# Attention and two feed-forward stages on one core: attention in the order of token thirds, with a table of times, and four pairs loaded in 1 KB runs

## The chip, the cores and the metric

One Trainium2 chip, one of its cores. The metric is the device time of one execution in microseconds. The kernel before was run three times; the median is 508.46 us (507.33 to 509.16).

## What is computed

Attention over q, k, v of shape (2, 8, 576, 64), float32, in two branches that are added. One averages q, k and v over groups of four tokens, does full softmax attention on 144 of them, and repeats each result four times. The other is local: each token sees the tokens less than 4 away. The sum, as 1152 tokens of 512 values, goes through two feed-forward stages, whose weights are float64 or float32 as the inputs have them:

```python
out = out_up + out_local                       # (2, 8, 576, 64)
x = out.transpose(0, 2, 1, 3).reshape(1152, 512)
h = x @ w_in                                   # 512 -> 2048
g = h * np.tanh(softplus(h))
y = g @ w_out                                  # 2048 -> 512
g2 = silu(y @ w_gate) * (y @ w_val)            # 512 -> 1536, twice
return g2 @ w_out2                             # 1536 -> 512
```

## The kernel before

**Names.** PE is TensorE, ACT ScalarE, DVE VectorE, POOL GpSimd, SP the engine that issues the transfers. Heads go in pairs: (b, p) is batch b, heads 2p and 2p + 1, eight pairs in all.

**The planner.** Nothing is issued in the order of the source. Each step is an `Op` with the engines that may do it and a guessed duration on each, the steps that it needs, the ring buffers that it takes, and a wanted time. `Plan.run` (line 97) plays the engines through in its own clock: an engine that is free takes, of the steps that are ready, the one with the smallest wanted time. The order found in this way is then issued, engine by engine, and each engine works through its own list in order. A wanted time is a priority and no time on the chip. Where PE has nothing ready before 95 us of the plan's clock, a dummy matmul (line 1082) is put in its list; it computes nothing that is used.

**prep** (line 396) takes one pair in. Tokens 0 to 511 of q and of k are loaded (lines 414 to 423) in runs of 256 B, so that one partition holds four neighbouring tokens of both heads, ordered token, head, value. The last 64 tokens come once for each batch (`ld_rem`, line 389), v in 1 KB runs (line 427), and POOL adds groups of four v rows (line 440). `t_main` (line 449) transposes four blocks of 128 x 128 for q and four for k (line 456), ACT evicts them (line 473), and DVE adds groups of four tokens (line 484). A branch for 1 KB runs stands in the code (lines 420 and 458 to 461) for batches named in `KB`, which is empty: one run holds four tokens of one head, and each block is a plain multiplication of one head's 64 columns with the identity.

**down** (line 505) is the averaged branch of one pair: score (520), maxima (525), exponentials on ACT (535), the scaling of the exponentials on ACT or DVE (548, 550), transposes (559), values (571). Its result goes to `up`.

**load_windows** (line 598) loads v for the local branch, a window of 70 tokens of four heads at a time (line 604), 36 in all.

**duo** (line 608) is the local branch of two units. A unit is (b, u, p): batch, third of its 576 tokens, pair. There are 24 units and 12 duos. Mask and scores (631, 636), maxima on DVE (642), exponentials on ACT (650), their sums either by ACT's accumulator or, with `late_sums`, by DVE (655), scaling (668), transposes (676), values (691). Then DVE adds the averaged branch (line 701), the sum is rounded to its high part (707) and the low part is taken (711); both go to `xt`.

**The first layer.** `convert` (line 265) loads one chunk of 512 KB of float64 weights and makes a high and a low float32 part of it: an absolute value on ACT or DVE (297, 299), four steps on DVE (303, 307, 312, 317), the high part on either (224 and 226 are the copy helper), the low part on DVE (333). `l1` (line 780) multiplies one chunk with one piece of 384 tokens (`cols_group`, 12 matmuls on lines 756 to 758). A piece is two thirds: piece 0 is the first two thirds of batch 0, piece 1 the last third of batch 0 and the first of batch 1, piece 2 the rest. An `l1` group needs every unit of its piece. For the first six chunks the three pieces are separate groups whose results are kept; `l2`, `l3` and `l4` follow in a fixed order.

**The order around the change** (lines 971 to 1050). `w` counts up by 4 a duo. The twelve duos are, by (b, u, p): 000+010, 001+011, 020+021, 002+012, 003+013, 022+023, 100+101, 110+120, 111+121, 102+103, 112+122, 113+123. Piece 0 so is complete after the fifth, piece 1 after the tenth, piece 2 after the twelfth. The first five have `late_sums`. Windows are asked for nine at a time. The weights' first conversion is wanted at

```python
    for f in range(WTS):
        convert("1", f, t_p0 + 4.5 * f, -4)
```

with t_p0 = 30, and `l1` of pieces 0, 1 and 2 from 40, 60 and 58 on.

Of the kernel before, what the change touches and what calls it, by code (L numbers as in the profile page):

```python
# [29 lines left out]
KB = ()  # L30
# [137 lines left out]
def attention_moe_kernel(  # L168
# [96 lines left out]
    def convert(kind, f, want, lead=None):  # L265
# [24 lines left out]
        if wide:  # L290
# [29 lines left out]
            o = plan.add({"ACT": us_act(512), "DVE": us_ts(512)}, mag, [o_load, prev.get("mag")], w0, [cw], [raw])  # L320
# [75 lines left out]
    def prep(b, p, w):  # L396
# [17 lines left out]
        def ld_main(i):  # L414
            def f(e):
# [33 lines left out]
        def t_main(i):  # L449
            def f(e):  # L450
# [3 lines left out]
                for r in range(4):  # L454
                    if b not in KB:
# [13 lines left out]
        def ev(i):  # L469
            def f(e):  # L470

                if i < 2:
# [16 lines left out]
        for i in range(3):  # L489
            o = plan.add({E_PE: ((1.06 if b in KB else 0.5) if i < 2 else 0.24)}, t_main(i) if i < 2 else t_rem,  # L490
# [4 lines left out]
            evs.append(plan.add({"ACT": us_act(n, True), **({} if 7 & 1 else {"DVE": us_tt(n)})}, ev(i), [o], w, use=[ps[i], qkT]))  # L495
# [4 lines left out]
        pairs[b, p] = dict(qkT=qkT, evs=evs, o_up=down(b, p, qkd, vd, o_d, o_v, w + 9.04+0.00))  # L500
# [4 lines left out]
    def down(b, p, qkd, vd, o_d, o_v, w):  # L505
# [37 lines left out]
        def weigh(h):  # L543
            def f(e):
                for c in range(2):
                    t, r = ed.tile[:, h, c], md.tile[:, 0, h, c:c + 1]
                    if e == "ACT":
                        ACT.activation(t, t, AF.Copy, scale=r)
                    else:
                        DVE.tensor_scalar(out=t, in0=t, scalar1=r, scalar2=None, op0=ALU.mult)  # L550
# [28 lines left out]
        o = add({E_PE: 0.54}, score, o_d, w, ba + [ed, md], [qkd])  # L579
        o = [add({"DVE": us_tt(2 * SD)}, mx(h), [o], w, use=[ba[h], md]) for h in range(2)]  # L580
        o = add({"DVE": 0.08}, neg, o, w, use=[md])
        o = add({"ACT": 1.25}, exps, [o], w, use=ba + [md, ed], table="exp")
        o = add({"DVE": 0.25}, norm, [o], w, use=[md])
        o_e = []
        for h in range(2):
            x = add({"ACT": 0.42, "DVE": 0.29}, weigh(h), [o], w, use=[md, ed])
            x = add({E_PE: 0.3}, turn(h), [x], w, [] if h else [ptd], [ed, ba[h]] + ([ptd] if h else []))
            o_e.append(add({"ACT": us_act(2 * SD, True)}, ev(h), [x] + o_e, w, use=[ba[h], ptd]))
        o = add({E_PE: 0.5}, values, o_e + o_v, w, use=[vd, ptd, ba[0]])
# [18 lines left out]
    def duo(units, ws, late_sums):  # L608
# [11 lines left out]
        xs = buf(wk, [128, 384], F32, "xs", 2)  # L620
        b_s, b_l = [bank() for _ in two], [bank() for _ in two]
        b_o = bank()

# [60 lines left out]
        def o_local(k):  # L684
            def f(e):
                if k == 0:
                    b_o.make()
                    xs.make()
                for j in range(3):
                    for h in range(2):  # L690
                        PE.matmul(out=b_o.tile[64 * h:64 * h + 64, 192 * k + 64 * j:192 * k + 64 * j + 64], lhsT=vw[k][j].tile[:, 2 * (units[k][2] % 2) + h],  # L691
                                  rhs=pt[k].tile[:, 128 * j + 64 * h:128 * j + 64 * h + 64], start=True, stop=True)
# [11 lines left out]

        hi, lo = [xt[:, z, p0:p0 + np_, 192 * s0:192 * (s0 + ns)] for z in range(2)]

        def x_hi(e):
            copy(e, hi, xs.tile.rearrange("p (c j) -> p c j", c=np_))

        def x_lo(e):  # L710
            DVE.tensor_tensor(out=lo, in0=xs.tile.rearrange("p (c j) -> p c j", c=np_), in1=hi.bitcast(F32), op=ALU.subtract)
# [7 lines left out]
        for k in two:  # L719
            pr, w, u = prs_[k], ws[k], units[k][1]  # L720
            o1 = add({E_PE: 0.66}, s_local(k), pr["evs"][:2 + (u == 2)] + [o_bf] + in_turn[-1:], w,
# [3 lines left out]
            o6.append(add({"ACT": 0.45 if late_sums else 0.92}, exps(k), [o3], w, [], [b_s[k], m, ex], "exp"))  # L725
# [15 lines left out]
        for k in two:  # L741
            o15.append(add({E_PE: 0.48}, o_local(k), [o12[k]] + o15 + l_w[k], w, [] if k else [b_o, xs],
                           [pt[k]] + vw[k] + ([b_o, xs] if k else [])))
        o17 = add({"DVE": us_tt(384)}, add_, o15 + [prs_[k]["o_up"] for k in two], w, use=[b_o, up, xs])
# [374 lines left out]
```

## Time and profile before

| what | us |
|---|---|
| median of three runs | 508.46 |
| the profiled execution's own time | 508.12 |
| its span, first to last instruction | 506.3 |
| PE recorded busy | 500.4 |
| DVE recorded busy | 351.3 |
| ACT recorded busy | 270.5 |

Times inside a profile count from the span's start. A matmul's recorded duration holds its way through the array, so durations of matmuls that follow one another overlap, and a stretch full of dummies is as busy as a stretch full of work. Where PE's true pace matters, it is read from how many instructions lie between two starts, or from the chain of waits, which counts no microsecond twice. A share of DMA is that of the 16 transfer engines.

### The profile page before, as it was taken

What the parts mean: (1) busy time and instruction counts of PE and PEld (TensorE: products, weight loads), DVE (VectorE), ACT (ScalarE), POOL (GpSimd) and SP (SyncE); (2) the same over time, 40 slices, a digit from 0 to 9 for tenths busy, and PEclk for the clock granted to TensorE, in tenths of its full rate; (3) what the DMA queues carried; (4) which work ended last, traced back from release to release, by engine and by line L of the source; (5) the groups of instructions that cost most, each with busy time, mean ns of one, the idle gap of its engine ahead of it and who ended that gap; (6) DMA issues with size and microseconds to landing.
All of it is one profiled execution on the core that took longest, in us unless ns stands there. A gap on an engine that the chain in (4) does not pass through costs nothing.

```text
span 506.3 us, 8742 instructions
## 1 busy us (share of the span) xinstructions
PE 500.4 (99%) x3387; PEld 469.3 (93%) x3387; DVE 351.3 (69%) x743; ACT 270.5 (53%) x602; POOL 24.7 (5%) x45
## 2 busy tenths in 40 slices
PE   9999999999999999999999999999999999999996
PEld 7777779999999999999999999999998899998885
DVE  3898999986966982877598986776763298622322
ACT  3989998699968860897053533344432444310000
POOL 4432220000000000000000000000000000000000
PEclk9999999999999999999999999999999999999999
DMA  9999533440451540045114252222222032000022
GB/s 174 197 168 220 147 102 101 149 132 15 123 174 34 167 128 39 1 126 167 41 43 124 88 162 85 85 83 85 83 84 83 1 124 84 1 1 0 1 96 90
DMA packets 58225, 48.23 MB, mean 95 GB/s; under 512 B 30664, under 2 KB 53448, under 8 KB 58184
## 3 DMA queue, kind: packets, MB, share of 16 engines
q1 hardware_dynamic: 58184, 47.68, 34.4%
q8 instruction: 26, 0.43, 0.4%
q14 instruction: 15, 0.12, 0.1%
HBM read 45.31 MB, written 2.36 MB: 94 GB/s over the span
## 4 chain that ended last, share of the span: by engine, by line
PE 91%; DVE 4%; ACT 3%; issue 1%; ACTq 0%
PE b L756 23%; PE b L757 23%; PE b L758 23%; PE b L943 5%; PE b L941 5%; PE b L942 5%; PE warm L1082 2%; PE b L691 1%; PE b L636 1%; PE b L456 1%; PE b L676 1%; DVE qkd L484 1%; ACT ex L650 1%; ACT ed L535 1%; PE b L520 1%
## 5 line engine op out<-in xcount | busy, mean ns | idle before, releaser
L756 PE MATMUL b<-xy,wt 128*128 128x384 f32 x480 | 161.2, 336 | 0.0
L758 PE MATMUL b<-xy,wt 128*128 128x384 f32 x480 | 160.4, 334 | 0.0
L757 PE MATMUL b<-xy,wt 128*128 128x384 f32 x480 | 160.4, 334 | 0.0
L756 PEld LDWEIGHTS b<-xy,wt 128*128 128x128 f32 x480 | 90.1, 188 | 0.4
L757 PEld LDWEIGHTS b<-xy,wt 128*128 128x128 f32 x480 | 90.1, 188 | 0.0
L758 PEld LDWEIGHTS b<-xy,wt 128*128 128x128 f32 x480 | 90.1, 188 | 0.0
L756 PE MATMUL b<-G,wt 128*128 128x384 f32 x192 | 64.1, 334 | 0.0
L757 PE MATMUL b<-G,wt 128*128 128x384 f32 x192 | 64.1, 334 | 0.0
L758 PE MATMUL b<-G,wt 128*128 128x384 f32 x192 | 64.1, 334 | 0.0
L224 ACT ACTIVATE G<-H 128x384 fp32r<-128x384 f32 (+1 forms) x38 | 21.7, 576 | 65.4 <-DVE H L913 44.5
L297 ACT ACTIVATE cw<-raw 128x512 f32<-128x512 f32 x65 | 43.7, 673 | 21.0 <-DVE wt L333 12.7
L333 DVE TENSOR_TENSOR wt<-cw,wt 128x512 fp32r<-128x512 f32 x68 | 46.2, 686 | 3.7 <-ACT wt L224 2.0
L312 DVE SCALAR_TENSOR_TENSOR cw<-raw,cw 128x512 uint32<-128x512 uint32 x68 | 46.5, 690 | 0.8
L317 DVE SCALAR_TENSOR_TENSOR cw<-raw,cw 128x512 uint32<-128x512 uint32 x68 | 46.5, 688 | 0.5
L943 PE MATMUL b<-wt,G 128*128 128x512 f32 x108 | 42.1, 389 | 0.0
L942 PE MATMUL b<-wt,G 128*128 128x512 f32 x108 | 42.0, 389 | 0.0
L941 PE MATMUL b<-wt,G 128*128 128x512 f32 x108 | 42.0, 389 | 0.0
L913 DVE TENSOR_TENSOR H<-b,H 128x384 f32<-128x384 f32 x36 | 19.9, 553 | 24.8 <-PE b L758 24.6
L956 DVE TENSOR_TENSOR acc<-b,acc 128x512 f32<-128x512 f32 x18 | 12.4, 692 | 34.6 <-PE b L943 34.6
L756 PEld LDWEIGHTS b<-G,wt 128*128 128x128 f32 x192 | 36.0, 188 | 0.0
L757 PEld LDWEIGHTS b<-G,wt 128*128 128x128 f32 x192 | 36.0, 188 | 0.0
L758 PEld LDWEIGHTS b<-G,wt 128*128 128x128 f32 x192 | 36.0, 188 | 0.0
(91 smaller groups left out, 690.2 us busy)
## 6 DMA issues: line engine op xcount, KB each, us to landing
raw<-in_moe_w_out_dram SPq DMA_DIRECT2D x28, 512.0 KB
raw<-in_moe_w_in_dram SPq DMA_DIRECT2D x16, 512.0 KB
raw<-in_moe_w_gate_dram SPq DMA_DIRECT2D x12, 512.0 KB
raw<-in_moe_w_val_dram SPq DMA_DIRECT2D x12, 512.0 KB
vw<-in_v_dram SPq DMA_DIRECT2D x36, 70.0 KB
vq<-in_v_dram SPq DMA_DIRECT2D x8, 288.0 KB
out_dram<-acc SPq DMA_DIRECT2D x9, 256.0 KB
qk<-in_q_dram SPq DMA_DIRECT2D x8, 256.0 KB
```

Source lines behind the costliest of these rows:

```text
L224: ACT.activation(out, in_, AF.Copy)
L297: ACT.activation(cw.tile, h.bitcast(F32), AF.Abs)
L312: DVE.scalar_tensor_tensor(out=c, in0=words()[:, :, 0], scalar=29, in1=c, op0=ALU.logical_shift_right, op1=ALU.bitwise_or)
L317: DVE.scalar_tensor_tensor(out=c, in0=words()[:, :, 1], scalar=0xC0000000, in1=c, op0=ALU.bitwise_and, op1=ALU.bitwise_or)
L333: DVE.tensor_tensor(out=wt.tile[:, 1], in0=cw.tile, in1=wt.tile[:, 0].bitcast(F32), op=ALU.subtract)
L756: PE.matmul(out=ps, lhsT=wt_hi, rhs=m_hi, start=first, stop=False)
L757: PE.matmul(out=ps, lhsT=wt_hi, rhs=m_lo, start=False, stop=False)
L758: PE.matmul(out=ps, lhsT=wt_lo, rhs=m_hi, start=False, stop=last)
L913: DVE.tensor_tensor(out=h.tile[:, cs], in0=pv.tile[:, 0:n], in1=h.tile[:, cs], op=ALU.mult)
L941: PE.matmul(out=ps.tile, lhsT=g[:, 0, tok], rhs=wt[:, 0], start=(f == fs[0]), stop=False)
L942: PE.matmul(out=ps.tile, lhsT=g[:, 0, tok], rhs=wt[:, 1], start=False, stop=False)
L943: PE.matmul(out=ps.tile, lhsT=g[:, 1, tok], rhs=wt[:, 0], start=False, stop=(f == fs[-1]))
```

## The change

The duos are put into another order, by thirds: 000+010, 001+011, 002+012, 003+013, then 020+100, 021+101, 022+102, 023+103, then 110+120, 111+121, 112+122, 113+123. Piece 0 is complete after the fourth, piece 1 after the eighth. All wanted times come from a table, `STEER`: for each prep its own (`p`) and those of its loads (`lm`, `lv`) and of `down` (`dn`); for each duo that of its two units (`d`, `d2`), whether DVE sums (`ls`), and whether the averaged branch is added on PE (`jn`, zero everywhere); for the window loads (`v`), which come as 6, 6, 3, 3, 3, 3, 6 and 6; for the first conversions (`c`) and the first-layer groups (`l`).

`kb` names four pairs, (0,0), (0,1), (1,0) and (1,2), whose q and k are loaded in 1 KB runs and multiplied with the identity. For pairs (0,0) and (0,3) (`ef`) the eviction of q and k may be done by DVE too. The scaling on DVE in `down` is one product with a broadcast factor in place of two scalings. The absolute value in `convert` is left to DVE alone, except for the gate and value weights and the first eight chunks of the first layer. Some of the planner's guessed durations are larger. The table, the helpers and the new order:

```diff
-KB = ()
+STEER = {
+    'p': [6.0, 10.9, 16.8, 21.5, 25.5, 31.2, 36.0, 43.6],
+    'lm': [-12.0, -12.0, -15.2, -11.8, -11.0, -10.5, -16.8, -11.6],
+    'lv': [-5.4, -4.3, -5.1, -2.0, -4.7, 1.2, -5.6, -5.0],
+    'dn': [-11.6, -14.7, -28.9, 0.0, 0.8, -17.7, -16.8, -1.3],
+    'ef': [1, 0, 0, 1, 0, 0, 0, 0],
+    'd': [8.6, 10.1, 21.8, 21.0, 25.5, 28.3, 37.1, 21.6, 42.8, 42.8, 55.6, 44.5],
+    'd2': [3.6, 1.6, 2.8, 5.0, 2.0, 4.2, 1.4, 3.2, 1.6, -0.6, 1.4, -3.2],
+    'ls': [0, 1, 1, 1, 0, 0, 0, 1, 1, 1, 0, 1],
+    'jn': [0, 0, 0, 0, 0, 0, 0, 0, 0, 0, 0, 0],
+    'v': [2.6, 17.4, 29.4, 31.1, 43.9, 28.4, 52.1, 40.3],
+    'c': [19.3, 29.9, 36.2, 38.3, 49.6, 57.4, 48.4, 63.9],
+    'l': [[46.8, 48.8, 48.3, 55.6, 57.8, 56.1], [62.0, 40.6, 65.3, 50.0, 71.2, 69.1], [35.7, 33.3, 27.8, 34.6, 36.5, 27.0]],
+    't': 65.5,
+    'kb': [1, 1, 0, 0, 1, 0, 1, 0],
+}
...
-            o = plan.add({"ACT": us_act(512), "DVE": us_ts(512)}, mag, [o_load, prev.get("mag")], w0, [cw], [raw])
+            o = plan.add({"DVE": us_ts(512), **({"ACT": us_act(512)} if kind in "gv" or (kind == "1" and f < WTS) else {})}, mag, [o_load, prev.get("mag")], w0, [cw], [raw])
...
-                if b in KB:
+                if STEER["kb"][4 * b + p]:
...
-            l_q.append(plan.add({E_SP: us_dma(256, 1024) if b in KB else us_dma(1024, 256)}, ld_main(i), l_q, w - 12, [] if l_q else [qk], [qk] if l_q else []))
-        l_v = [plan.add({E_SP: us_dma(288, 1024)}, ld_v, [], w - 5, [vq])]
+            l_q.append(plan.add({E_SP: us_dma(256, 1024) if STEER["kb"][4 * b + p] else us_dma(1024, 256)}, ld_main(i), l_q, w + STEER["lm"][4 * b + p], [] if l_q else [qk], [qk] if l_q else []))
+        l_v = [plan.add({E_SP: us_dma(288, 1024)}, ld_v, [], w + STEER["lv"][4 * b + p], [vq])]
...
+                if i < 2 and e == "DVE":
+                    DVE.tensor_scalar(out=qkT.tile[:, i, 0:512].rearrange("p (j r) -> p j r", r=4),
+                                      in0=ps[i].tile.rearrange("p (r j) -> p j r", r=4), scalar1=(0.125, 1.0)[i], scalar2=None,
+                                      op0=ALU.mult)
...
+                if e == "DVE":
+                    t = ed.tile[:, h]
+                    DVE.tensor_tensor(out=t, in0=t, in1=md.tile[:, 0, h].unsqueeze(2).to_broadcast([72, 2, SD]), op=ALU.mult)
+                    return
...
+    prep(0, 0, STEER['p'][0])
+    load_windows(0, 0, range(0, 6), STEER['v'][0])
+    duo([(0, 0, 0), (0, 1, 0)], (STEER['d'][0], STEER['d'][0] + STEER['d2'][0]), STEER['ls'][0], bool(STEER['jn'][0]))
...
     for f in range(WTS):
-        convert("1", f, t_p0 + 4.5 * f, -4)
-    for i, t in enumerate((t_p0, t_p1, t_p2)):
+        convert("1", f, STEER["c"][f], -4)
+    for i in range(3):
         for f in range(RING):
-            l1(f, i, t + (10, 10, 0)[i] + f * ((t_p1 - t_p0) / RING if i == 0 else (t_p2 - t_p1) / RING if i == 1 else GROUP_US))
+            l1(f, i, STEER["l"][i][f])
...
-    t = t_p2 + RING * GROUP_US + -7.24
+    t = STEER["t"]
```

## Rows read from the trace of the kernel before

**Rows 1.** Part 1 of the page: engine, busy us, share of the span, instructions.

```profile
PE 500.4 (99%) x3387; PEld 469.3 (93%) x3387; DVE 351.3 (69%) x743; ACT 270.5 (53%) x602; POOL 24.7 (5%) x45
```

**Rows 2.** Busy us of each engine (x instructions) by stretch, PEclk, DMA share, GB/s.

```profile
0.00:10.00 10.00, 8.82 (x76) 7.14 (x77) 2.06 (x6) 3.45 (x8) 4.73 (x21) 1.00 0.94 166
...
20.00:30.00 10.00, 9.77 (x162) 7.62 (x161) 8.58 (x25) 8.48 (x37) 4.34 (x6) 1.00 1.16 185
...
70.00:80.00 10.00, 10.00 (x129) 8.06 (x125) 9.75 (x31) 9.60 (x39) 0.00 (x0) 1.00 0.29 78
...
130.00:506.30 376.30, 372.53 (x2049) 359.49 (x2048) 242.22 (x471) 160.62 (x264) 0.00 (x0) 1.00 0.25 80
```

**Rows 3.** Line 1082's group in the whole span, 30 to 93 us, 42 to 93 us.

```profile
L1082 PE MATMUL warm<-wsrc 128*128 128x256 bf16 x103 | 16.5, 297 | 1.2 <-DVE wsrc L375 1.2
...
L1082 PE MATMUL warm<-wsrc 128*128 128x256 bf16 x41 | 6.9, 275 | 0.0
...
42.00:93.00 51.00, 5.64 (x34) 2.55 (x32) 1.00 0.52 130
```

**Rows 4.** The chain of waits in order of time, first 40 us: start, us, what.

```profile
1.18 3.59 PE warm L1082 x16
...
5.43 1.09 PE warm L1082 x10
...
9.85 0.44 PE b L456 x4
...
12.06 0.60 PE b L456 x4
...
34.93 0.64 PE b L571 x8
...
36.93 1.03 PE b L456 x8
```

**Rows 5.** As rows 2, two other stretches.

```profile
2.50:5.00 2.50, 2.50 (x14) 1.94 (x13) 0.00 (x0) 0.00 (x0) 2.18 (x8) 1.00 1.10 245
...
330.00:350.00 20.00, 20.00 (x118) 20.00 (x117) 14.06 (x28) 7.32 (x14) 0.00 (x0) 1.00 0.32 100
```

**Rows 6.** DVE's time line (start, us, instruction), all of line 701, PE's time line.

```profile
48.05 0.56 DVE L701 TENSOR_TENSOR xs<-b,up 128x384 f32<-128x384 f32 x1 [0.31 <-PE b L691]
...
50.73 0.43 DVE L303 TENSOR_SCALAR cw<-cw 128x512 f32<-128x512 f32 x1 [0.39 <-ACT cw L297]
...
57.12 0.68 DVE L333 TENSOR_TENSOR wt<-cw,wt 128x512 fp32r<-128x512 f32 x1
...
L701 DVE TENSOR_TENSOR xs<-b,up x12: 537/550/558, 26.2 to 92.0; 128x384 f32<-128x384 f32 x12
...
57.80 0.42 PE L756 MATMUL b<-xy,wt 128*128 128x384 f32 x1
```

**Rows 7.** DVE's time line and PE's, first 10 us.

```profile
6.07 0.21 DVE L370 CAST identb<-ident 128x128 bf16<-128x128 f32 x1
...
7.96 0.58 PE L636 MATMUL b<-qkT 64*64 64x70 f32 x12
```

**Rows 8.** Groups of instructions by line: count, busy us, mean ns, idle before.

```profile
L655 DVE TENSOR_REDUCE m<-ex 128x6 f32<-128x420 f32 x5 | 2.9, 577 | 0.0
...
L650 ACT ACTIVATION_READ_ACCUMULATOR ex<-b,m 128x1 f32 x42 | 8.9, 212 | 0.0
...
L550 DVE TENSOR_SCALAR ed<-ed,md 72x144 f32<-72x144 f32 x18 | 4.7, 308 | 0.0
...
L299 DVE TENSOR_SCALAR cw<-raw 128x512 uint32<-128x512 uint32 x3 | 1.3, 423 | 0.2 <-DMA raw<-in_moe_w_val_dram 0.2
```

**Rows 9.** SP's time line: issues of loads.

```profile
14.91 4.99 SPq L604 DMA_DIRECT2D vw<-in_v_dram  x9
...
20.00 0.61 SPq L422 DMA_DIRECT2D qk<-in_q_dram  x1
```

**Rows 10.** PE's waits by releaser: us in total, times, longest.

```profile
PE b L676 <- ACT ex L650: 0.2, 1, 0.2
```

More of the change, by code (lines that the diff above doesn't have):

```diff
@@ L494, in prep @@
             n = 512 if i < 2 else 128
-            evs.append(plan.add({"ACT": us_act(n, True), **({} if 7 & 1 else {"DVE": us_tt(n)})}, ev(i), [o], w, use=[ps[i], qkT]))
+            evs.append(plan.add({"ACT": us_act(n, True), **({"DVE": us_tt(n)} if i < 2 and STEER["ef"][4 * b + p] else {})}, ev(i), [o], w, use=[ps[i], qkT]))
         o_d = []
@@ L577, in keep @@
             ACT.activation(up.tile[:, p, SD * b:SD * b + SD], ba[0].tile[:, 2 * SD:3 * SD], AF.Copy, scale=0.25)
-        o = add({E_PE: 0.54}, score, o_d, w, ba + [ed, md], [qkd])
+        o = add({E_PE: 0.65}, score, o_d, w, ba + [ed, md], [qkd])
         o = [add({"DVE": us_tt(2 * SD)}, mx(h), [o], w, use=[ba[h], md]) for h in range(2)]
         o = add({"DVE": 0.08}, neg, o, w, use=[md])
-        o = add({"ACT": 1.25}, exps, [o], w, use=ba + [md, ed], table="exp")
+        o = add({"ACT": 1.43}, exps, [o], w, use=ba + [md, ed], table="exp")
         o = add({"DVE": 0.25}, norm, [o], w, use=[md])
@@ L606, in load_windows, with duo @@
             wins[b, y, t] = (vw, plan.add({E_SP: us_dma(4 * WIN, 256)}, f, [], w, [vw]))
-    def duo(units, ws, late_sums):
+    def duo(units, ws, late_sums, joined):
         LW = 3 * WIN
@@ L687, in f @@
                     b_o.make()
-                    xs.make()
+                    if not joined:
+                        xs.make()
                 for j in range(3):
@@ L691, in f @@
                         PE.matmul(out=b_o.tile[64 * h:64 * h + 64, 192 * k + 64 * j:192 * k + 64 * j + 64], lhsT=vw[k][j].tile[:, 2 * (units[k][2] % 2) + h],
-                                  rhs=pt[k].tile[:, 128 * j + 64 * h:128 * j + 64 * h + 64], start=True, stop=True)
+                                  rhs=pt[k].tile[:, 128 * j + 64 * h:128 * j + 64 * h + 64], start=True, stop=not joined,
+                                  skip_group_check=joined)
             return f
@@ L741, in duo @@
         for k in two:
-            o15.append(add({E_PE: 0.48}, o_local(k), [o12[k]] + o15 + l_w[k], w, [] if k else [b_o, xs],
-                           [pt[k]] + vw[k] + ([b_o, xs] if k else [])))
-        o17 = add({"DVE": us_tt(384)}, add_, o15 + [prs_[k]["o_up"] for k in two], w, use=[b_o, up, xs])
-        o18 = add(flex(us_act(384), us_ts(384), 8), x_hi, [o17], w, use=[xs])
-        o19 = add({"DVE": us_tt(384)}, x_lo, [o18], w, use=[xs, flight])
+            o15.append(add({E_PE: 0.48}, o_local(k), [o12[k]] + o15 + l_w[k], w, [] if k else acc,
+                           [pt[k]] + vw[k] + (acc if k else [])))
+        u_ops = [prs_[k]["o_up"] for k in two]
+        if joined:
+            o17 = add({E_PE: 0.66}, join, o15 + u_ops, w, use=[b_o, up])
+            o18 = add({"ACT": us_act(384, True), "DVE": us_tt(384)}, x_hi, [o17], w, use=[b_o])
+            o19 = add({"DVE": us_tt(384)}, x_lo, [o18], w, use=[b_o, flight])
+        else:
+            o17 = add({"DVE": us_tt(384)}, add_, o15 + u_ops, w, use=[b_o, up, xs])
+            o18 = add(flex(us_act(384), us_ts(384), 8), x_hi, [o17], w, use=[xs])
+            o19 = add({"DVE": us_tt(384)}, x_lo, [o18], w, use=[xs, flight])
         for b, u, p in units:
@@ new lines, in attention_moe_kernel @@
+    prep(0, 2, STEER['p'][2])
+    load_windows(0, 1, range(0, 6), STEER['v'][1])
+    duo([(0, 0, 2), (0, 1, 2)], (STEER['d'][2], STEER['d'][2] + STEER['d2'][2]), STEER['ls'][2], bool(STEER['jn'][2]))
+    prep(0, 3, STEER['p'][3])
+    duo([(0, 0, 3), (0, 1, 3)], (STEER['d'][3], STEER['d'][3] + STEER['d2'][3]), STEER['ls'][3], bool(STEER['jn'][3]))
+    prep(1, 0, STEER['p'][4])
+    load_windows(0, 0, range(6, 9), STEER['v'][2])
+    load_windows(1, 0, range(0, 3), STEER['v'][3])
+    duo([(0, 2, 0), (1, 0, 0)], (STEER['d'][4], STEER['d'][4] + STEER['d2'][4]), STEER['ls'][4], bool(STEER['jn'][4]))
```

89 lines of the change are left out of this document (33 added, 56 removed).

## The prediction, written before the changed kernel ran

> **What bounds the kernel now.** I read the page first. TensorE (PE) is recorded busy for nearly the whole span [rows 1], so the question is where that record hides idle time. The table of stretches answers half of it [rows 2]: after 130 us PE is busy 372.53 of 376.3 us, and what is missing lies after its last matmul. VectorE (DVE) is busy there for 242.22 us only. Nothing done to attention can help or hurt in that stage unless it adds PE work or pushes DVE up by half. At 70 to 80 us the table looks different: DVE 9.75 and ScalarE (ACT) 9.60 of 10, so three engines are near full at once. In the first 10 us DVE and ACT have a great deal of room.
>
> Then the dummies [rows 3, 4]. Line 1082 issues matmuls that compute nothing, wherever the plan has no work for PE. There are 103. The first 16 cover 3.59 us, later ones cost 1.09 us for ten, 0.109 each. Between 30 and 93 us 41 of them ran: 4.5 us. 34 of the 41 stand behind 42 us. That leaves 103 - 16 - 41 = 46 between 4.8 and 30 us: 5.0 us. With the 1.18 us before the first one, 1.2 + 3.6 + 5.0 + 4.5 = 14.3 us of the first 92 are no work. This is nearly the whole stock from which the change can take.
>
> The chain shows what the dummies wait for [rows 4]. Up to 12 us it is transposes of freshly loaded q and k with dummies between them: the loads. Then it runs through DVE and ACT for a while. The transfers are saturated in that time: a share of 1.1 or so of the 16 engines, from 2.5 us to past 25, at 245 GB/s at first and some 185 later [rows 2, 5].
>
> Last, the first layer's start [rows 6]. The first group of line 756 runs at 57.80 us. Two things end there. The fifth of twelve attention units (the last one that the first third of tokens needs) writes its sum at 48.05 us, and the first weight chunk, begun on DVE at 50.73, is finished by line 333 at 57.80. The twelve sums lie between 26.2 and 92.6 us, (92.0 - 26.2) / 11 = 6.0 us apart, which is the pace of DVE.
>
> **The change part by part.** *Order by thirds.* The first third of the tokens now needs four units instead of five, the second eight instead of ten; the last still needs twelve. At 6 us a unit, groups of the first layer can start about 6 us sooner, and those of the second third 12 us sooner, if the weights are there; the table asks for the first weight conversion 19.3 + 4 us into the plan, where it was 30 + 4, some 11 us sooner. One group is 12 matmuls of 20.00 / 118 = 0.17 us [rows 5], 2.0 us, and 12 groups of the first two thirds are 24 us: far more than the 4.5 us of dummies after 30 us that they can replace. Bounds: nothing (weights late), or 4.5 plus about 0.5 of small gaps. I take **-4.0**, nearer the upper end, since filler becomes available at 48 - 6 = 42 us and 34 of the 41 dummies stand behind that [rows 3].
>
> *1 KB runs for four pairs of eight.* Eight loads of 256 KB change. At 20 to 30 us, mostly 256 B runs, a share of 1.16 moved 185 GB/s [rows 2]: 160 at a share of 1, so 1.64 us a load. Weight loads at 330 to 350 us, in runs of 1 KB and more, moved 100 GB/s with 0.32 [rows 5]: 312, so 0.84 us. Each load is worth 0.8 us of transfer time. Four of them are the first two pairs, at the very start, where the queue is what PE waits for: 3.2 us. The first score cannot move that far, because the mask is ready only at 6.28 us and the score stood at 7.96 [rows 7]: 1.7 at most. The second pair, transposed at 9.85 and 12.06 us [rows 4], can move by the whole. DVE and ACT have room before 15 us, and from there on they set a pace of 6 us a unit, so an earlier start moves that pace as a whole. Bounds 0 and -3.2; I take **-2.5**. The other four loads are at a time when DVE holds the pace: 0, hidden behind DVE; without that cover another 3.2 to win.
>
> The same edit costs PE time. A transposed 128-column block is one instruction, eight of them 1.03 us [rows 4], four 0.52. In the new layout each head's 64 columns are multiplied with the identity: 8 multiplications per load, which the trace records as two instructions each. The nearest row is line 571, also 64 stationary columns with outputs on alternate halves: eight instructions of 144 columns in 0.64 us [rows 4], so 16 of 128 columns take 16 x 0.08 x 128/144 = 1.14 us, 0.6 more than now. If a plain multiplication cost the full slot of a transpose per instruction (0.13), it would be 2.1 us, 1.6 more. I take 0.6: eight loads make 4.9 us. The first four displace dummies before 20 us, 0; were those gone, 2.4. The last four lie where I have just filled the dummies with real work: **+2.4** on the path, between 0 (if dummies are left there after all) and 6.4.
>
> The Trainium skill speaks against this edit: "FP8 and Floating Point Precision", TensorE Precision Notes, gives true FP32 four passes through the array, so a block would cost four times a transpose. By it eight would take 4.2 us a load without overlap, and the sum would end near 522. The trace does not agree for line 571: a 144-column multiplication takes 0.16 us there, about 1.1 times a transpose of as many columns. The measurement decides.
>
> *Small edits.* Two more units sum the exponentials on DVE: 2 x 0.58 on DVE against 12 x 0.21 on ACT [rows 8]. Line 550's two scalings of 0.26 become one product of 288 columns, under the 0.55 that 384 columns take [rows 6, 8]: some tenths of a microsecond over nine of them, either way. Evictions of two pairs may go to either engine. Together 0 within 1 us, covered by the other of the two engines. The absolute value of 36 of 68 weight chunks moves to DVE for good: at most 36 x 0.42 = 15 us, nearly all after 90 us; behind 130 us DVE had 134 us of 376 to spare [rows 2, 8]: 0 behind PE; uncovered it would be 15. No unit uses the joined path, so it costs nothing.
>
> *Queues.* The value windows come as 6, 6, 3, 3, 3, 3, 6, 6 instead of four times 9. Nine held SP for 4.99 us at 14.91, with the next q load behind them at 20.00 [rows 9]; six let it through about 1.7 us sooner, but two pairs more are asked for early. The vector sums on POOL follow their loads and had waits of their own. I count 0, within 1.
>
> The sum: -4.0 - 2.5 + 2.4 = -4.1. The profiled execution took 508.12 us (span 506.3 and 1.8 around it), 0.34 under the median of the three runs. So 504.0 in its terms and **504.4 us** against the median of 508.46.
>
> **The rivals.** *Gains eaten (no change).* DVE and ACT take no earlier start over, since all three engines are near full later on, and the four late loads cost their 2.4: -2.5 of filling, 0 of the front, +2.4, about 508.3. For it: DVE at 9.75 of 10 [rows 2]. Against: DVE's 2.06 in the first 10 us.
>
> *PE stands for weights (slower).* PE works in order. A first-layer group that the plan puts ahead of a chunk still in work stops the scores and transposes queued behind it, and DVE then has nothing to reduce. The first chunk took 7.1 us from its first DVE step to its last for 2.9 us of work (two steps of 0.43, three of 0.68), as attention lay between [rows 6]. Pulled 11 us forward, into the densest part, the first three chunks late by 2.5 us each cost 7.5: -4.1 + 7.5 = +3.4, 511.9. It decides from 4.1 us of such waits on. For it: the first group ran right at the end of line 333, with nothing to spare. Against: PE's waits for DVE and ACT inside attention are three, 0.2 us each [rows 10], so the plan's guess of durations was close.
>
> *Deeper gain.* The whole stock after 5 us that is within reach goes: -3.2 of loads, -5.0 of dummies and gaps, and the late identity multiplications fall into what were waits: -8.2, 500.3.
>
> *Four passes.* A multiplication that doesn't transpose takes four times a transpose's slot [rows 4], one head after the other: 8 x 4 x 0.13 = 4.2 us a load, 3.6 more than now, 29 for eight. At most 8.6 of that lies under the dummies before 30 us: 29 - 8.6 - 6.5 = +14, 522. It is what the page named above would make of it. For it: no row shows this very form. Against: line 571.
>
> **How the numbers follow.** Forecast 0.48, deeper gain 0.14, gains eaten 0.18, PE stands for weights 0.17, four passes 0.03. About 0.3%, 1.5 us, is what a measurement here can tell from no change. Faster is 0.48 + 0.14 = 0.62, the same 0.18, slower 0.20. The range takes in the deeper gain and most of the waiting case: 500.2 to 510.8. The forecast's own is 502 to 506.5.
>
> **What would show it.** Right: the first group of the first layer before 50 us; under 20 dummies after 30 us; the second pair's transposes done by 10 us; an identity load near 1.1 us; the twelfth sum before 90 us. Wrong: PE idle with a weight as its releaser, DVE under 9 of 10 between 40 and 80 us with PE waiting, or the last attention unit later than 92 us with as many dummies as before.

## The result, and the profile after

The changed kernel takes **512.40 us** (median of 13 runs, 508.49 to 514.81) against 508.39 for the kernel before, run beside it: a ratio of 1.0071 [1.0055, 1.0087]. It is slower by 4 us, where 4 us less were forecast; the range missed it too. The profiled execution took 513.18 us with a span of 511.4, 5.1 more than the span before.

Part 1 of the page shows PE as busy as before. ACT has 53 us less to do than in [rows 1], DVE 8.5 more:

```profile
PE 501.6 (98%) x3422; PEld 470.4 (92%) x3422; DVE 359.8 (70%) x766; ACT 217.4 (43%) x531; POOL 23.3 (5%) x45
```

PE's waits by releaser (us in total, times, longest); `vw` is a window of v, `ed` and `ex` are the exponentials of `down` and of the local branch. Before, no wait but that of 1.2 at the start was above 0.2 [rows 10]:

```profile
PE b L713 <- DMA vw<-in_v_dram: 2.4, 2, 2.2
PE warm L1104 <- DVE wsrc L391: 1.2, 1, 1.2
PE b L579 <- DVE ed L567: 1.0, 1, 1.0
PE b L476 <- DMA qk<-in_k_dram: 0.6, 1, 0.6
PE b L472 <- ACT qkT L497: 0.5, 1, 0.5
PE b L697 <- DVE ex L689: 0.2, 1, 0.2
```

The stretches, with the columns of [rows 2], to be read against its second and third last numbers, PEclk and the share of DMA:

```profile
30.00:40.00 10.00, 7.57 (x97) 5.65 (x95) 6.88 (x19) 7.08 (x30) 4.34 (x6) 0.91 1.01 191
40.00:50.00 10.00, 10.00 (x96) 8.29 (x95) 6.65 (x17) 5.03 (x19) 2.16 (x3) 0.58 0.96 193
50.00:60.00 10.00, 8.99 (x128) 7.40 (x127) 9.83 (x27) 8.80 (x43) 2.90 (x3) 1.00 0.74 171
...
130.00:511.40 381.40, 377.59 (x2079) 364.54 (x2077) 247.35 (x493) 122.41 (x220) 0.00 (x0) 1.00 0.25 78
...
36.00:38.00 2.00, 0.83 (x12) 0.59 (x12) 1.59 (x5) 0.29 (x1) 0.53 (x1) 1.00 0.91 172
38.00:40.00 2.00, 2.00 (x20) 1.46 (x20) 2.00 (x5) 1.21 (x3) 0.00 (x0) 0.55 1.18 193
40.00:42.00 2.00, 2.00 (x26) 1.67 (x26) 1.05 (x2) 0.99 (x3) 0.00 (x0) 0.50 1.07 173
...
48.00:50.00 2.00, 2.00 (x13) 1.76 (x12) 0.90 (x3) 1.68 (x7) 0.00 (x0) 0.89 0.83 221
```

After 130 us PE lacks 381.40 - 377.59 = 3.8 us, as before [rows 2]: nothing changed there. At 38 us the granted clock drops from 1.00 to 0.50, the lower of its two levels (1.2 GHz of 2.4), and it returns at about 48 us. A record that says PE was busy for all of 40 to 50 us hides this: 96 instructions ran, where experiment 3, below, has 129 in the same stretch.

PE's time line shows what came before the fall, and the signs that the prediction named:

```profile
8.40 2.17 PE L476 MATMUL b<-ident,qk 128*64 128x128 f32 x32
...
31.95 1.92 PE L476 MATMUL b<-ident,qk 128*64 128x128 f32 x32
33.80 0.34 PE L483 MATMUL b<-ident,qr 64*128 64x64 f32 x2
...
36.94 0.69 PE L713 MATMUL b<-pt,vw 70*64 70x64 f32 x8 [2.16 <-DMA vw<-in_v_dram]
37.84 0.34 PE L713 MATMUL b<-pt,vw 70*64 70x64 f32 x4 [0.20 <-DMA vw<-in_v_dram]
...
47.22 1.65 PE L472 MATMUL b<-ident,qk 128*128 128x128 f32 x8
...
49.07 0.44 PE L790 MATMUL b<-xy,wt 128*128 128x384 f32 x1
```

Value products (line 713, 691 before) stand 2.16 us for a window of v. Eight transposes that took 1.03 us [rows 4] take 1.65, the last of them at the higher clock again. The groups of the dummies and of the sums on DVE (duration min/median/max in ns, first and last start in us), and the second sum on DVE's time line:

```profile
L1104 PE MATMUL warm<-wsrc x42: 272/282/422, 1.2 to 47.0; 128*128 128x256 bf16 x42
...
L724 DVE TENSOR_TENSOR xs<-b,up x12: 524/550/558, 27.4 to 102.1; 128x384 f32<-128x384 f32 x12
...
28.19 0.55 DVE L724 TENSOR_TENSOR xs<-b,up 128x384 f32<-128x384 f32 x1
```

103 dummies became 42 [rows 3], and none is left after 47 us. Yet the last sum comes at 102.1 us instead of 92.0 [rows 6]. SP's time line says where the late windows were:

```profile
20.81 0.62 SPq L436 DMA_DIRECT2D qk<-in_q_dram  x1
21.48 0.46 SPq L436 DMA_DIRECT2D qk<-in_k_dram  x1
22.04 0.38 SPq L443 DMA_DIRECT2D vq<-in_v_dram  x1
22.46 1.50 SPq L438 DMA_DIRECT2D qk<-in_q_dram  x1
24.01 1.91 SPq L438 DMA_DIRECT2D qk<-in_k_dram  x1
26.02 3.65 SPq L443 DMA_DIRECT2D vq<-in_v_dram  x1
29.72 0.40 SPq L296 DMA_DIRECT2D raw<-in_moe_w_in_dram  x1
30.17 4.00 SPq L624 DMA_DIRECT2D vw<-in_v_dram  x6
```

The two issues at 20.81 and 21.48 are q and k of pair (1,2), which PE first reads at 55.86 us. Behind them stand another pair, two loads of v, whose second issue held SP for 3.65 us where the first took 0.38, and a weight chunk. Only then come the six windows. In the chain of waits the third of them, the last that the waiting product needs, is in transfer from 31.78 us for 6.01, until PE goes on at 37.84. DVE stood as well, for that weight chunk, with attention's next scaling (line 689) behind it in its queue; DVE's time line:

```profile
36.35 0.46 DVE L315 TENSOR_SCALAR cw<-raw 128x512 uint32<-128x512 uint32 x1 [2.32 <-DMA raw<-in_moe_w_in_dram]
36.73 0.36 DVE L689 TENSOR_TENSOR ex<-ex,m 128x210 f32<-128x210 f32 x1
```

**An account of PE's time** that is not work of the kernel before, from these rows. A dummy behind the first ones counts 0.109 us [rows 4]. An identity load takes 1.05 us in the front (8.40 to 10.50 for two) and 0.93 later (31.95 to 33.80), where transposes take 0.52: 4 x 0.53 + 4 x 0.41 = 3.8. Half a clock costs half the time: (1 - 0.55) x 2 + (1 - 0.58) x 10 = 5.1 from 38 to 50 us. The last column is experiment 7, below, in which both stands are cured; its four other waits are 0.7, 0.6, 0.5 and 0.2.

| us | before | after | exp. 7 |
|---|---|---|---|
| to the first dummy | 1.2 | 1.2 | 1.2 |
| first dummies (16, 12, 12) | 3.6 | 2.7 | 2.7 |
| other dummies (87, 30, 44) | 9.5 | 3.3 | 4.8 |
| PE's other waits | 0.6 | 4.7 | 2.0 |
| identity beyond transposes | 0 | 3.8 | 3.8 |
| half clock | 0 | 5.1 | 0 |
| sum | 14.9 | 20.8 | 14.5 |
| span | 506.3 | 511.4 | 506.4 |

The sums differ by +5.9 and -0.4, the spans by +5.1 and +0.1: the account holds within 1 us.

### The profile page after: what moved, and what is told of

It reads as the page before. It is cut to its first block, busy times and chain, and to the rows that moved or that the text cites. A ratio compares the mean times of both kernels' runs of the same rounds, so it can differ in the third digit from the quotient of the medians.

```text
span 511.4 us, 8727 instructions
## 1 busy us (share of the span) xinstructions
PE 501.6 (98%) x3422; PEld 470.4 (92%) x3422; DVE 359.8 (70%) x766; ACT 217.4 (43%) x531; POOL 23.3 (5%) x45
## 4 chain that ended last, share of the span: by engine, by line
PE 92%; DVE 3%; SPq 2%; DMA 2%; issue 1%; ACT 0%; DVEq 0%
PE b L790 23%; PE b L792 23%; PE b L791 23%; PE b L976 5%; PE b L977 5%; PE b L975 5%; PE b L657 2%; PE b L713 2%; DMA vw<-in_v_dram 1%; PE b L697 1%; DMA qk<-in_k_dram 1%; SPq L443 1%; PE b L540 1%; PE b L472 1%; SPq L438 1%; PE b L476 1%
## 5 line engine op out<-in xcount | busy, mean ns | idle before, releaser
L240 ACT ACTIVATE G<-H 128x384 fp32r<-128x384 f32 (+1 forms) x40 | 24.0, 606 | 66.6 <-DVE H L947 45.7
L904 DVE TENSOR_TENSOR acc<-b,acc 128x384 f32<-128x384 f32 x36 | 19.8, 554 | 23.6 <-PE b L792 23.6
```

What stands on the lines that cost most here:

```text
L240: ACT.activation(out, in_, AF.Copy)
L904: DVE.tensor_tensor(out=ya, in0=ps.tile[:, 0:n], in1=ya, op=ALU.add)
```

## The experiments

Theory A: windows late through SP's order make PE stand, and the stand takes the clock down. Rivals: the transfers are the limit, whatever their order; the stand matters and not the clock; a single part of the change (order, 1 KB runs, table) carries the loss. No experiment changes what is computed; they differ in the order of issues, in dummies, or in the layout of loads. `move` takes issues out of the order that the plan found and puts them back elsewhere; `fill(step, n)` puts n dummies ahead of a step on PE. Ratios are against the kernel before, run beside each.

**1. Windows ahead of pair (1,2)** (SP's order alone).

```diff
+        move(lambda t: t[:3] == ("vw", 0, 1) and t[3] < 6, before=lambda t: t == ("qk", 1, 2))
```

> The changed kernel with one edit on SP's queue alone: the six value windows of pairs 2 and 3, batch 0 (asked for at 17.4 in the table) are issued ahead of the q and k loads of pair (1,2) instead of behind them, behind pair (1,1)'s and behind a weight chunk. Lists of all other engines are unchanged. Theory (PE stands for these windows for 2.2 + 0.2 us, and the TensorE clock falls after that stand): no wait of line 713 for windows, granted clock 1.00 throughout, 2.4 + 5 us less than the changed kernel, 504 to 506. Rival 1 (the clock falls for another reason, as the dummies are fewer): wait gone, clock still near 0.99, 509 to 511. Rival 2 (the transfers are the limit, so that what is put behind the windows comes late in its turn: POOL's vector sums, the first weight chunk): another wait of 1 to 3 us in the same place, 507 to 511.

515.40 us, 1.0133 [1.0103, 1.0163]: worse. PE's longest wait, then DVE's time line:

```profile
PE b L714 <- DVE ex L706: 5.0, 2, 4.8
```

```profile
38.91 0.63 DVE L330 TENSOR_SCALAR cw<-raw 128x512 uint32<-128x512 uint32 x1 [5.47 <-DMA raw<-in_moe_w_in_dram]
39.46 0.36 DVE L706 TENSOR_TENSOR ex<-ex,m 128x210 f32<-128x210 f32 x1
```

The windows are in time; what was moved back is late now. The weight chunk lands so late that DVE, in order, stands 5.47 us, and PE 4.8 us behind it; the granted clock is 0.50 from 40 to 50 us. So the rival of saturated transfers holds for this order: with the windows first, others are late. This is also the nearest that a run came to the rival "PE stands for weights", though it is DVE that stands for them.

**2. Pair (1,2) behind the windows**, the one load that nobody needs soon.

```diff
+        move(lambda t: t == ("qk", 1, 2), after=lambda t: t[:3] == ("vw", 0, 1) and t[3] < 6)
```

> The changed kernel with one edit on SP's queue alone: the q and k loads of pair (1,2), which PE needs at 56 us only, go behind the six value windows that PE waits for at 35 us; the windows so move up by two loads of 256 KB, some 2 us. Theory (the stand is a matter of the order of transfers): the wait of 2.4 us falls under 0.7, the clock stays at 1.00, 504 to 507. Rival 1 (the clock falls for another reason): 509 to 511. Rival 2 (transfers as a whole are too slow): the wait keeps more than half of its length or moves to pair (1,2), 508 to 512.

509.20 us, 1.0021 [0.9998, 1.0045]: 3.2 us of the loss gone by the medians, 2.5 by the ratios. PE's waits, then stretches:

```profile
PE b L595 <- DVE ed L583: 1.8, 2, 1.2
...
PE b L730 <- DMA vw<-in_v_dram: 0.2, 1, 0.2
```

```profile
40.00:50.00 10.00, 10.00 (x119) 8.09 (x120) 9.90 (x30) 8.48 (x38) 2.71 (x3) 1.00 0.98 213
...
54.00:56.00 2.00, 1.52 (x12) 1.33 (x13) 2.00 (x6) 1.31 (x6) 0.00 (x0) 0.70 0.96 263
56.00:58.00 2.00, 2.00 (x19) 1.43 (x19) 2.00 (x5) 1.44 (x4) 0.00 (x0) 0.50 0.06 20
```

The window's wait is 0.2 us and the clock stays up to 50 us. A later stand of 1.2 us, for DVE's scaled exponentials of `down`, is followed by a shorter fall.

**3. Dummies in the wait**: the order of the changed kernel, 20 dummies ahead of the first late value product, so that PE doesn't stand.

```diff
+        fill(("ol", 0, 0, 2), 20)
```

> The changed kernel with 20 dummy matmuls (2.2 us of PE) put into PE's list right ahead of the first value product of pair 2, the instruction that stands 2.2 us for its windows. The transfers are not touched. Theory (it is the stand that takes the clock down): the wait stays, filled, the clock stays at 1.00, about 5 us less than the changed kernel: 507 to 508.5. Rival 1 (the clock has no part in it or falls for another reason): within 1 us of the changed kernel, clock near 0.99.

511.30 us, 1.0060 [1.0033, 1.0086]. Stretches of its profiled execution (510.82 us):

```profile
40.00:50.00 10.00, 10.00 (x129) 8.24 (x129) 9.93 (x26) 8.62 (x37) 2.71 (x3) 1.00 1.02 197
...
56.00:58.00 2.00, 1.63 (x13) 1.42 (x14) 2.00 (x5) 1.37 (x6) 0.00 (x0) 0.74 0.88 251
58.00:60.00 2.00, 2.00 (x20) 1.46 (x20) 2.00 (x5) 1.33 (x4) 0.00 (x0) 0.50 0.10 29
```

With work that means nothing in the place of the stand, the clock holds from 30 to 50 us: the fall needs the idle PE, not the late window. The stand ahead of 56 us, 1.4 us for `ed`, was followed by a fall instead. Four of the ten runs had a mean clock of 0.99 like the changed kernel's, and the median hardly gained.

**4. The kernel before with the four pairs in 1 KB runs**, its orders kept.

```diff
+KB4 = ((0, 0), (0, 1), (1, 0), (1, 2))
-                if b in KB:
+                if (b, p) in KB4:
```

> The kernel before, all its orders kept, with q and k of the same four pairs loaded in 1 KB runs and multiplied with the identity. Theory (an identity load takes 0.93 us of PE against 0.52, so 1.6 us for the two late pairs, and the first two pairs come earlier by some 1.5 to 2.5 us): 507 to 508.5, no change or slightly faster. Rival (the identity multiplications are what made the changed kernel slower): 510 to 512.

511.15 us, 1.0055 [1.0034, 1.0076]: +2.8 us. The first block starts at 4.71 us behind the same 16 dummies, then ten more stand ahead of k. Data that land sooner can't pass dummies that the order holds. The sums run from 28.7 to 95.4 us [rows 6]: 2.5 us late at the first and 3.4 at the last.

**5. The changed kernel with all pairs in 256 B runs**, its orders kept.

```diff
-                if STEER["kb"][4 * b + p]:
+                if False:
```

> The changed kernel, every engine's order kept, with all eight pairs loaded in 256 B runs and transposed in blocks as before; only the form of the loads and of their transposes differs. Theory (the transfers run behind what the plan believes, so longer loads make the stands longer): 8 x 0.41 = 3.3 us less PE work, but the stand for the windows grows from 2.4 us to 4 or more and the clock falls at least as far, 512 to 516. Rival (the identity multiplications are the cause of the loss): 3 us less than the changed kernel, 508.5 to 510.

514.73 us, 1.0149 [1.0103, 1.0195], 2.3 us above the changed kernel: the transfers it saves are worth more than the identity costs, in a plan that counts on them. PE now waits 1.7 us for q, 2.2 for windows and 2.0 for `ed`.

**6. Both stands filled**: experiment 3 and 14 dummies ahead of the turn of pair (1,1).

```diff
+        fill(("ol", 0, 0, 2), 20)
+        fill(("turn", 1, 1, 0), 14)
```

> The changed kernel with 20 dummies ahead of the first value product of pair 2 (as in the run with one stand filled) and 14 more ahead of the transposes of the averaged branch of pair (1,1), where PE stood 1.4 us for DVE's scaling in that run and the clock fell to 0.5. No transfer is touched. Theory (each stand takes the clock down by itself, and filled stands don't): clock 1.00 in all stretches, 508 to 509.5, 3 to 4.5 us under the changed kernel. Rival (the clock falls for want of work, not of busy time): the clock still falls near one of the two places, 510.5 to 512.

508.71 us, 1.0027 [1.0011, 1.0043]. Stretches:

```profile
30.00:40.00 10.00, 9.09 (x120) 7.33 (x119) 5.85 (x18) 6.62 (x30) 3.85 (x5) 1.00 0.84 159
40.00:50.00 10.00, 9.69 (x122) 7.95 (x124) 9.93 (x26) 8.42 (x35) 2.71 (x3) 1.00 1.01 207
50.00:60.00 10.00, 10.00 (x150) 8.10 (x146) 9.93 (x26) 8.43 (x37) 3.06 (x4) 1.00 0.86 189
```

Nothing was moved and nothing comes sooner; PE only has 34 more useless matmuls. All seven runs have a mean clock of 0.999 or 1.0, where ten of the changed kernel's thirteen have 0.99 or less. That is worth 512.40 - 508.71 = **3.7 us** by the medians and 2.2 by the ratios: the price of the falls.

**7. Pair (1,2) back, and the second stand filled.**

```diff
+        move(lambda t: t == ("qk", 1, 2), after=lambda t: t[:3] == ("vw", 0, 1) and t[3] < 6)
+        fill(("turn", 1, 1, 0), 14)
```

> The changed kernel with pair (1,2)'s q and k loads behind the six windows, and 14 dummies ahead of the transposes of the averaged branch of pair (1,1). Theory: no wait for windows, no fall of the clock at 54 us; the run without the dummies lost 4.6 us at half clock in its profile (2.3 us of work) and took 509.2: 506.5 to 508, at or just under the kernel before. Rival (the dummies cost what the clock gives): 508.7 to 510.

508.76 us, 1.0018 [1.0002, 1.0033]. With no long stand and no fall, the change still gains nothing. Three of its stretches:

```profile
40.00:50.00 10.00, 9.95 (x115) 8.04 (x117) 9.90 (x30) 8.38 (x38) 2.70 (x3) 1.00 1.04 227
...
70.00:80.00 10.00, 10.00 (x124) 8.56 (x122) 9.90 (x31) 8.55 (x31) 0.00 (x0) 1.00 0.54 149
...
110.00:130.00 20.00, 20.00 (x117) 20.00 (x116) 20.00 (x35) 16.03 (x23) 0.00 (x0) 1.00 0.19 53
```

DVE is at 9.6 to 10 of 10 from 30 to 130 us. The dummies taken out went into identity work and waits, by the table above.

**8. The order by thirds alone**, put into the kernel before with wanted times counted up as before.

```diff
-    duo([(0, 2, 0), (0, 2, 1)], (w, w + 2.0), True)
...
+    duo([(0, 2, 0), (1, 0, 0)], (w, w + 2.0), True)
```

> The kernel before with the order by thirds alone: the twelve duos, the preps and the windows in the changed kernel's sequence, but wanted times that count up by 4 a duo as before, the planner's old guesses, 256 B runs throughout, DVE's sums in the first five duos. Theory (the order by thirds asks for all eight pairs in eight duos instead of ten while the transfers are full, so the plan's lists stand for transfers): PE waits of 1 to 3 us in attention and a fall of the clock, 510 to 515. Rival (the order itself is a gain, as forecast, and the table spoils it): no waits, 504 to 507.

516.04 us, 1.0162 [1.0147, 1.0177]. There are 153 dummies, and the first sum is at 36.9 us instead of 26.2. With it came another order on SP: the first six windows are issued at 24.71 us, where nine were at 14.91 [rows 9]. So this run shows what the order costs with such wanted times, and not what it costs by itself. One wait, then the stretches around it:

```profile
PE b L559 <- ACT ed L548: 1.4, 1, 1.4
```

```profile
54.00:56.00 2.00, 1.05 (x11) 0.77 (x9) 1.97 (x8) 0.57 (x1) 0.00 (x0) 1.00 0.45 75
56.00:58.00 2.00, 1.49 (x14) 1.24 (x15) 0.04 (x1) 2.00 (x11) 0.00 (x0) 1.00 0.96 286
```

A stand of 1.4 us here, and no fall.

**9. Experiment 7 with pairs (1,0) and (1,2) in 256 B runs.**

```diff
-                if STEER["kb"][4 * b + p]:
+                if STEER["kb"][4 * b + p] and b == 0:
```

> The run with pair (1,2)'s loads put back and the 14 dummies (508.76 us), with pairs (1,0) and (1,2) loaded in 256 B runs and transposed again; the first two pairs keep 1 KB. Theory (without stands, identity multiplications are paid in full, 0.41 us for each of four loads, as nothing on PE is left that they could displace): 1.6 us less, 506.8 to 507.8, under the kernel before. Rival (DVE, 9.9 of 10 busy from 30 to 110 us in that run, sets the end, so PE work is free): within 0.7 us of 508.76. Rival 2 (pair (1,0)'s longer loads push the windows behind them late again): a wait for windows and 509.5 or more.

511.73 us, 1.0065 [1.0043, 1.0088], 3.0 us above experiment 7 by the medians, 2.4 by the ratios. Eight of the ten runs have a mean clock of 0.99 or less; the profiled one, at 509.98 us, is not among them and has a shorter fall (0.83 from 40 to 50 us). PE waits 1.5 us for scaled exponentials there, and for no load. So the late 1 KB loads are worth something, and in which way is not shown.

**10 and 11. Fewer early dummies in the kernel before**, up to 12 at first and 4 at each later place before 30 us (28 fewer in PE's list by the traces, where the expectations say 31); in 10 the first two pairs in 1 KB runs as well.

```diff
+                if x[0] < 30.0 and n > (12 if x[0] < 6.0 and not any(y[2] == "PE" and y[1] is not self.spare[0] for y in kept) else 4):
+                    continue
...
+KB2 = ((0, 0), (0, 1))
```

> The kernel before with the first two pairs in 1 KB runs, and with fewer dummies in PE's list up to 30 us: at most 12 ahead of the first work and at most 4 in each later place, 31 fewer. All other orders kept. Theory (dummies are instructions that are worked off in order, so earlier data cannot pass them; with them out, the early identity loads cost nothing and the front comes forward): 505.5 to 507.5. Rival (the front hangs on the chain of ACT and DVE, and the identity multiplications are paid, or PE stands and the clock falls): 508.5 to 511.

> The kernel before with the same 31 dummies out and nothing else. Theory (data comes when it comes: the places of the dummies become waits for loads, with no stand over 1 us): 507 to 508.5, the clock at 1.00. Rival 1 (dummies held PE up): 505 to 507. Rival 2 (the gaps take the clock down): 509.5 or more, clock under 0.995.

10: 508.89 us, 1.0007 [0.9991, 1.0023]. 11: **506.42 us**, 0.9953 [0.9934, 0.9972], faster than both kernels. The groups of the twelve sums, first 10, then 11:

```profile
L711 DVE TENSOR_TENSOR xs<-b,up x12: 537/550/558, 26.4 to 92.7; 128x384 f32<-128x384 f32 x12
```

```profile
L710 DVE TENSOR_TENSOR xs<-b,up x12: 540/550/559, 26.7 to 91.6; 128x384 f32<-128x384 f32 x12
```

With the early 1 KB loads the first sum comes 0.3 us sooner, the second 0.9 us later (31.2 against 30.3) and the last 1.1 us later. What the front wins is gone at the second sum, and 2.5 us of the median are lost.

The profiled execution of 11 is the slowest of its ten (507.71), and PE's time line shows a likely reason. Four dummies take 1.06 us near 7 us and 0.60 near 13, though the granted clock is given as 1.00 from 0 to 20 us:

```profile
7.25 1.06 PE L1091 MATMUL warm<-wsrc 128*128 128x256 bf16 x4
...
13.15 0.60 PE L1091 MATMUL warm<-wsrc 128*128 128x256 bf16 x4
```

Their starts are 0.215 and 0.11 us apart; in the kernel before, the first 16 dummies take 0.22 each and the later ones 0.109 [rows 4]. So the front ran at the lower level up to about 9.7 us, and the granted clock does not show it at the start of a trace.

**12. A plan that lets loads land later**, which asks for them in time by itself.

```diff
-                o.end = free[e] + (2.2 if e == "SP" else 0.0)
+                o.end = free[e] + (4.5 if e == "SP" else 0.0)
```

> The changed kernel with one number of the planner changed: a transfer's data is taken to be there 4.5 us after its issue, not 2.2 (in the changed kernel's trace the windows landed 3.6 to 6.8 us after theirs). The first run of dummies stays at 12. Theory (the stand comes from lists that were made for transfers which land sooner than they do): the stand for windows goes or falls under 1 us, clock 0.997 or more, 507 to 509.5. Rival (the transfers' order is at fault, whatever the plan believes of their landing): a stand of over 1 us for windows or weights stays, 510.5 to 513.

511.53 us, 1.0049 [1.0022, 1.0076]. The longest wait is 0.8 us in the profiled run, which is the fastest (509.06) and held clock 1.00; its waits are many and small, 3.7 us in all behind the start. In six of the ten the mean clock was 0.992 or less, and what took it down there no trace shows.

**13. The changed kernel planned for 256 B runs.**

```diff
-    'kb': [1, 1, 0, 0, 1, 0, 1, 0],
+    'kb': [0, 0, 0, 0, 0, 0, 0, 0],
```

> The changed kernel with kb zero for all pairs in the table, so that the planner makes its lists for 256 B loads and block transposes; order by thirds, times and all else as changed. Its PE list has 94 dummies where the changed kernel's has 42. Theory (the order and the table gain nothing once their own waits and dummies are counted; 1 KB runs cost 3.3 us of PE and let the plan drop dummies): no gain over the kernel before, 508.5 to 514. Rival (thirds and table are a gain and the 1 KB runs spoil it): 504 to 507.5.

512.37 us, 1.0064 [1.0039, 1.0089], as the changed kernel. Two of its runs kept a mean clock of 1.0 and took 511.96 and 512.77: order and table bring nothing without the 1 KB runs, even at full clock. The trace has 106 dummies (the expectation says 94), some 35 of them after 30 us: with this order and table, the plan drops its dummies only where it counts on 1 KB runs.

**14. At most two dummies at a place** in the kernel before.

```diff
+                if n > (2 if began else 12):
+                    continue
```

> The kernel before with at most 12 dummies ahead of the first work and at most two in any later place, over all 95 us of the plan; nothing else. Theory (a dummy is an instruction that PE works off in order, 0.109 us each, and most stand where PE's next work is ready already): a little under the run that lost 31 of them, 505.5 to 506.5, the clock at 0.998 or more. Rival (they hold the clock up): stands of over a microsecond, clock under 0.995, 508.5 or more.

**506.10 us**, 0.9963 [0.9936, 0.9990]; three of ten runs lie between 508.9 and 511.2. The profiled one, at 509.63, is one of these. A stretch of it, with a stand of 1.2 us for ACT:

```profile
16.00:18.00 2.00, 1.08 (x12) 0.61 (x12) 1.93 (x7) 1.84 (x9) 1.55 (x3) 1.00 1.07 218
```

The clock holds here, and the mean clock is 0.998 or more in all ten runs. Near 10.6 us four transposes take 1.06 us where they take 0.66 from 13.5 us on, so the front ran at the lower level for longer than in experiment 11. Whether that is what slows three of the runs is not shown. As good as experiment 11 at the median, less sure.

**15. A stand in the kernel before**: two weight chunks ahead of nine windows.

```diff
+        move(lambda t: t in (("raw", "1", 0), ("raw", "1", 1)), before=lambda t: t[:3] == ("vw", 0, 1))
```

> The kernel before with one edit on SP's queue alone: the first two weight chunks (1 MB) are issued ahead of the nine windows of pairs 2 and 3, batch 0, that PE needs at 41 us, so that PE stands for them as it does in the changed kernel. Theory (a stand of some 2 us costs its own length and a fall of the clock to half for some 10 us, in whatever kernel): a wait of 1.5 to 4 us on line 691's windows, granted clock 0.5 in stretches after it, 512 to 517. Rival (the fall of the clock is peculiar to the changed kernel's lists): the same wait, clock 1.00, 509.5 to 512.

509.08 us, 1.0010 [0.9989, 1.0030]. The largest new wait is 0.6 us: no stand was made in the profiled run, so it tells nothing of the clock. One of the ten runs, without a trace, took 513.41 us at a mean clock of 0.992.

## Why the prediction was wrong

The sign was wrong, through two steps and one thing that no step held.

**"Queues ... I count 0, within 1"** is the step that failed first. The prediction saw that "two pairs more are asked for early", and that nine windows had held SP for 4.99 us [rows 9], and set one against the other. With the transfers saturated [rows 2], a load asked for 35 us ahead of its use delays one that is due. Six windows moreover held SP for 4.00 us, and not for six ninths of 4.99. The stand was 2.4 us, and experiment 2, which moves that load alone, takes back most of the loss (3.2 of 4.0 us by the medians, 2.5 of 3.6 by the ratios).

**The clock** stood in none of the sums. Every row of before has a granted clock of 1.00, and the dummies were counted as stock alone. They also keep PE from standing. The change takes 61 of them out, PE stands, and ten microseconds run at the low level. Experiment 6 shows the price, 3.7 us of 4.0 by the medians and 2.2 of 3.6 by the ratios. Fewer dummies are not enough for it: the kernel before lost 55 in experiment 14 and kept its clock. The spread of the changed kernel goes with it: its three runs at 0.997 or more took 508.5 to 510.6 us, the ten at 0.99 or less 511.7 to 514.8.

**"1 KB runs ... I take -2.5"** failed too. The second pair's turn is over at 10.5 us, 2.2 us sooner than [rows 4], as forecast. Of the sums the second follows (28.2 us instead of 31.1) and the first doesn't (27.4 after 26.2). Experiments 10 and 11 show it without the rest of the change: 0.3 us ahead at the first sum, behind from the second on. "An earlier start moves that pace as a whole" is what fell. Instead the early loads cost 2.5 us there, near the 2.4 that the prediction gave four loads with no dummies left to displace. The other four, counted 0 behind DVE, were worth 3.0 (2.4 by the ratios) in experiment 9, what the clock lost included.

**"The first four displace dummies ... 0"** is wrong where the order stays. A dummy is an instruction of the list like any other, and a longer load of identity work comes on top of it (experiment 4: +2.8 for all eight loads). In the changed kernel's own list they did displace some: 62 dummies up to 30 us became 35. The size was nearly right: 0.53 and 0.41 us a load beyond the transposes, where 0.6 was taken.

The Trainium skill, "FP8 and Floating Point Precision", TensorE Precision Notes, by whose four passes such a load would take an estimated 4.2 us, is not borne out by the 1.05 and 0.93 us here.

**"Order by thirds ... -4.0"** came in its own terms in the changed kernel. The first group of the first layer ran at 49.07 us instead of 57.80 [rows 6], at 43.50 in experiment 7, and 41 dummies after 30 us became 7: 34 x 0.109 = 3.7 us. It is not the order's alone, since some 35 are left with the same order and table in experiment 13. It was spent again: 3.8 on identity work, 1.4 on new waits in experiment 7, with DVE full. That DVE's being full is why nothing was left is argued from its stretches and not shown by a run of its own.

The pace, "6 us a unit" (its units are the duos), did not hold. The first-layer groups of the second third were to start 12 us sooner, with the eighth sum in place of the tenth. The tenth came at 82.2 us before, the eighth at 83.1 in the changed kernel and at 78.1 in experiment 7. By thirds, all eight pairs fall to the first eight duos, where the kernel before has ten for them.

**Small edits** were 0 after 130 us, where PE lacks as little as before. Up to there DVE has 3.4 us more to do ((359.8 - 247.4) - (351.3 - 242.2)), and what part these edits have in that is not shown; the product on line 567 takes 542 ns in the mean where two scalings took 2 x 0.26 us [rows 8].

**The rivals.** "PE stands for weights" had the right shape: an instruction in order, ahead of its data, and others queued behind it. It named the wrong data; no first-layer group waited in PE for a weight. That its 511.9 us lies near the 512.40 measured is luck, as the half clock had no part in its sum. "Gains eaten", at 508.3, is what is left when the stands are cured (508.7 and 508.8). Of the signs, the first group before 50 us, the count of dummies and the price of an identity load came out right. The second pair was done at 10.5 us instead of 10. Of the signs of a wrong forecast, two came in half: DVE at 6.65 of 10 from 40 to 50 us, with PE at half clock and not waiting, and the twelfth sum at 102.1 us, with 42 dummies and not 103.

**Still open**: what decides whether a stand takes the clock down, and whether one would in the kernel before, where experiment 15 made none. Even runs of one and the same kernel differ: of the changed kernel's thirteen, three were at 0.997 or more.

## What to carry to other kernels

When dummies go, ask what will stand in their place: count the waits, and read the granted clock in stretches of 2 us, since a busy share of 10 of 10 can be half speed; at the start of a trace read the pace of the instructions themselves. Where transfers are saturated, sort loads by when they are needed, and look at the queue for a load that is early at the cost of one that is due. Filler in a fixed order doesn't give way to data that come early; taking some of it out of the kernel before made it about 2 us faster, which the whole change did not.

## What was not expected of the hardware

- The length of a stand did not tell whether the clock fell, in one trace for each kernel. Falls followed 2.2 us (the changed kernel, experiment 5), 1.4 (experiment 3), 1.2 (experiment 2) and 0.7, with another of 0.4 two microseconds ahead of it (experiment 13, 0.72 from 40 to 50 us). None followed 1.0 (the changed kernel, at 59 us), 1.4 (experiment 8) and 1.2 (experiment 14).
- The same identity load took 1.05 us in the front and 0.93 us behind 30 us, at a granted clock of 1.00 both times.
- One issue of 288 KB on SP took 0.38 us at 22 us and 3.65 us at 26 us, with the share of DMA at 1.04 from 20 to 30 us: an issue of the same size can hold its engine nearly ten times as long. What it waited for is not shown.
- 28 dummies of the front of the kernel before, by [rows 4] four at 3.59 / 16 and 24 at 0.109 us, 3.5 in all, gave about 2 us back when they were taken out (experiment 11: 506.42 against 508.39 and, beside it, 508.80).
